# Batch 0 of an attention and snake-MLP kernel: the last pair's V by heads, two first-layer tiles opened early, w_in in five loads

## The chip, the cores and the metric

The kernel runs on one core of one Trainium2 chip. A core has TensorE (PE in the profile; PEld are its weight loads), VectorE (DVE), ScalarE (ACT), GpSimd (POOL) and SyncE (SP), and 16 DMA engines. The metric is device microseconds of one execution. The median of three timed runs of the kernel before is 215.98 us (215.56 to 216.43).

## The reference

An attention over short windows, then a feed-forward layer with the snake function, in float32:

```python
# 4 batches, 8 heads, 768 rows, 64 columns a head; 8 memory rows a head
for c in range(24):                       # chunks of 32 rows
    q_c    = q[:, :, 32*c : 32*c+32]
    k_full = concat(mem_k, k[:, :, max(0, 32*c-16) : min(768, 32*c+40)])
    v_full = concat(mem_v, v[...the same rows...])
    a = softmax(q_c @ k_full.T / 8)
    out[:, :, 32*c : 32*c+32] = a @ v_full
x = out.transpose(0, 2, 1, 3).reshape(3072, 512)
h = x @ w_in                              # 512 -> 2048
g = h + sin(alpha * h)**2 / (alpha + 1e-9)
return g @ w_out                          # 2048 -> 512
```

## The kernel before

Matmuls are in bfloat16. One program works through the four batches, 768 rows each, in five stages. Stage -1 does the attention of batch 0 alone. Stage i (0 to 3) does the feed-forward layer of batch i and beside it the attention of batch i+1. There is no planner at run time: the order of the whole program is written out by hand as strings of short words, and `Stage.run` (L525) calls for each word the method `do_` and its first letter. Each engine gets its instructions in this order and works through them in order; the waits between engines come from the data and the buffers.

The words that matter here, for batch 0 (its attention works by pairs of heads, 0 to 3, and by halves of 384 rows):

- `Vbhk` (L637, `load_v` L160): POOL issues the loads of V of batch b, heads h to k-1, into `vw`: L172 for 64 rows and L179 for 56 rows of each window of 96 queries, with 8 windows ("blocks") a head; for head 0 of batch 0 also L168. `dm` (L665) loads mem_v; `m0` copies it into `vw` (L188).
- `sph` (`u_scores`, L314): scores of pair p, half h: two matmuls for the mask (L317), eight for q·k (L325), then one exp on ACT (L332) into one of eight `pt` buffers.
- `vph` (`u_values`, L339): eight matmuls of the weights with V (L344), for two heads and four windows; then `normed` (L350): a reciprocal (L353) and one multiplication (L354, 96x512) on DVE into a slot `x_blk`.
- `Tph` or `tph` (`turned`, L362): four transposes on TensorE (L366) and a copy into `xT` (L369), on ACT for `T` and on DVE for `t`.
- `Ws` (`warm`, L698): a one-element Sin on ACT (L699), which makes it load the Sin table there.
- `Ixy` (`load_w_in`, L212): POOL issues the load of w_in for the first-layer tiles x to y-1 (digits above 9 as letters, g is 16), 128 columns a tile, 128 KB a tile as stored; the instruction is at L213. `Uxy` does the same for w_out (L219); `dq108`, `dk108` load q and k of batch 1 (L155).
- `bn`, `hn` (L546, L552): the two halves of first-layer tile n, four matmuls each (`half_tile`, L422, the instruction is L424), one for each 128 rows of w_in; the row block kt of w_in goes with pair kt of `xT`. `h` then has ACT take the Sin (L439). `qnE`: the square on ACT (L444), DVE or POOL (L447). `gn`: DVE makes the tile of `gT` (L451), and the tile's two PSUM banks are given back.
- `pn`, `Pn` (L540, L543, `early` L533): open tile n with the matmuls of kt 0 to 2 alone, for the first and the second half; a later `b` and `h` do what is left. The strings of before do not use them.
- `fn`: n matmuls of the second layer (L462) from a feed; `zn`: n matmuls of zeros (L686) that have no use as data.

PSUM has eight banks, handed out by `Banks` (L59): a score tile, a value tile and a first-layer tile take two neighbours, a transposed tile one; the oldest ones given back are taken first. So four first-layer tiles fill it, and the fifth waits for the first `g`.

In stage -1 before, the pairs come in the order 1, 0, 3, 2. V of the last pair (heads 4 and 5) is loaded by `V046`, after `m0`.

Of the kernel before, what the change touches and what calls it, by code (L numbers as in the profile page):

```python
# [9 lines left out]
P = 128  # L10
QW = 96
# [4 lines left out]
F32 = mybir.dt.float32  # L16
ACTF = mybir.ActivationFunctionType
ALU = mybir.AluOpType
# [67 lines left out]
def kernel(  # L86
# [12 lines left out]
    nc = tc.nc  # L99
    B, H, S, D = q.shape  # L100
# [4 lines left out]
    HP = H // 2  # L105
# [3 lines left out]
    HALF = S // 2  # L109
# [6 lines left out]
    blk = ctx.enter_context(tc.tile_pool(name="blk", bufs=3))  # L116
# [4 lines left out]
    banks = Banks(ps)  # L121
# [11 lines left out]
    vws = [consts.tile([P, H, NJ, VP], BF, name=f"vw{i}") for i in range(2)]  # L133
    xslots = Slots([consts.tile([QW, HP, 2, D], BF, name=f"x_blk{i}") for i in range(6)])
# [204 lines left out]
    def u_values(b, hp, half, pt):  # L339
        ot, bs = banks.pair()  # L340
        otv = ot[:, :, 0:4 * (D + 1)].rearrange("p e (g c) -> p e g c", c=D + 1)
        for e in range(2):
            for i in range(4):
                nc.tensor.matmul(  # L344
                    otv[:, e, i, :], pt[:, HALF * e + QW * i:HALF * e + QW * i + P],
                    vws[b % 2][:, 2 * hp + e, 4 * half + i, 0:D + 1],
                )
        return normed(otv, bs)

    def normed(otv, bs):  # L350
        rinv = blk.tile([QW, 2, HP], F32, name="rinv")
        x_blk = xslots.take()
        nc.vector.reciprocal(rinv[:], otv[0:QW, :, :, D])  # L353
        nc.vector.tensor_tensor(  # L354
            out=x_blk[:].rearrange("p g e d -> p e g d"), in0=otv[0:QW, :, :, 0:D],
            in1=rinv[:].unsqueeze(3).to_broadcast([QW, 2, HP, D]),
            op=ALU.mult,
        )
        banks.give(bs)
        return x_blk  # L360

    def turned(x_blk, out, eng):  # L362
        bank, bs = banks.single()
        xtp = bank[:, 0:2 * QW].bitcast(BF).rearrange("p (g c) -> p g c", g=4)
        for g in range(4):
            nc.tensor.transpose(  # L366
                xtp[:, g, :], x_blk[:, g].rearrange("p e d -> p (e d)"), ident[0:QW, 0:QW]
            )
        copier(eng)(out, xtp)  # L369
        banks.give(bs)  # L370

    def u_turn(xT, hp, half, x_blk, eng="V"):
        turned(
            x_blk,
            xT[:, hp, HALF * half:HALF * half + HALF].rearrange("p (g c) -> p g c", g=4), eng)
# [32 lines left out]
    def values(b, j, pt):  # L408
        ot, bs = banks.pair()
        otv = ot[:, :, 0:4 * (D + 1)].rearrange("p e (g c) -> p e g c", c=D + 1)  # L410
        for e in range(2):
            for hp in range(HP):
                i = 4 * e + hp
                nc.tensor.matmul(  # L414
                    otv[:, e, hp, :], pt[:, QW * i:QW * i + P],
                    vws[b % 2][:, 2 * hp + e, j, 0:D + 1],
                )
        return normed(otv, bs)
# [84 lines left out]
    class Stage:  # L503
# [99 lines left out]
        def do_v(self, a):  # L603
            if self.b == 0:
                self.xb[a] = u_values(0, int(a[0]), int(a[1]), self.pt.pop(a))
            else:
                self.xb[a] = values(self.b, int(a), self.pt.pop(int(a)))

        def turn_x(self, a, eng):
            x = self.next_x()  # L610
            x_blk = self.xb.pop(a)
            if self.b == 0:
                u_turn(x, int(a[0]), int(a[1]), x_blk, eng)
            else:
                turned(x_blk, x[:, :, QW * int(a):QW * int(a) + QW], eng)
            xslots.give(x_blk)
# [186 lines left out]
    def const_s():  # L803
# [7 lines left out]
    stage = Stage(-1, None)  # L811
    stage.tile = first
    stage.run((
        'a1A Cb Cp Cz Cv a5A eVA Cm Cl z4 a0V Ci k0 dm a4V l0 k1 K0V Ck l1 L0A V024 We L1V a2A K1A V002 '
        'a6V k2 s00 K2V a3V s11 V068 m0 a7V s01 l2 s10 k3 K3A L2A V046 z4 v10 l3 Cs L3A I02 v11 s20 z1 '
        'v01 s30 z1 v00 s31 z1 v30 s21 v31 T01 T10 v20 T30 T00 v21 T20 T31 I27 t11 t21 eVA Ws '
    ))
    for i, words in enumerate(((
        'o8 b0 h0 I7g q0V U69 U12 b1 h1 dq108 q1A b4 h4 b3 g0 h3 b6 g1 dk108 q4V g4 q3A b2 h2 h6 b5 h5 '
        'Ufg g3 b7 q2V U01 U56 q6P h7 g2 q5A b10 U24 q7P g6 h10 b9 q10A g5 h9 U45 b8 h8 g7 g10 q8A q9V '  # L820
        'V158 b11 h11 g9 b13 g8 h13 l0 l2 l3 L0A L2A q13P k2 q11V Ube b15 U9b g11 Uef g13 K2V h15 b12 '
        'q15V h12 q12A b14 g15 f7 h14 V125 k1 k0 g12 l1 K1V k3 L1V L3A q14V K3A K0A V102 f9 g14 s61 f16 '
        'm1 s70 s3 f13 v0 f3 v6 c6 f6 v3 f5 s542 T3 f10 T0 v4 f6 v2 f2 v1 c4 c2 f7 v7 f1 T1 f3 v5 Ws T7 '
        'f8 t5 '
    ),(
        'b0 o1 h0 b3 R2 q0V h3 b1 Ws q3A g0 g3 h1 q1V b2 R4 h2 q2A b5 h5 b4 h4 Ws g1 g2 q5V g5 b6 q4A h6 '
        'R8 Ws g4 b8 q6A g6 h8 R1 b9 q8V dy h9 b7 q9A g8 Z h7 R3 V378 b11 h11 b10 g9 V226 h10 R4 q7V Ws '
        'q10A f2 X8 q11A g7 f8 b12 h12 g10 g11 b14 h14 q12P g12 b13 h13 V202 q13A g13 q14A f7 X6 b15 g14 '
        'h15 f7 eV We s24 q15V f6 g15 f7 V268 s05 s1 f1 m2 f14 v4 v1 f6 v0 f1 v2 f2 c4 f6 s63 s7 t1 f4 c2 '
        'v6 V357 T0 f4 v3 f4 v7 c7 v5 t3 f17 t5 T6 '  # L830
    ),(
        'b3 Ws R9 b0 h0 R1 h3 b5 h5 Ws R1 b1 q5A q0V g0 R2 q3P g3 h1 Ws q1A b2 h2 g5 R1 g1 b4 h4 R1 b6 '
        'q4A q2V h6 g2 R1 Z b7 h7 b9 h9 R1 g4 R2 q6V b8 g6 R1 eV o1 h8 q7P g7 q8A b11 h11 X1 q11A q9P b10 '
        'g9 g8 h10 b13 g11 h13 q10V g10 b14 h14 b12 q13P X3 V305 h12 g13 q12V q14A R1 f8 eAV b15 g12 '
        'R1 H3 h15 f6 g14 q15V X8 s24 f16 g15 f2 s103 f9 v4 v0 f3 X1 f2 X1 c4 v3 f2 c3 v2 f1 c2 f6 c0 '
        's675 f10 v1 f4 c1 Ws f1 v7 v5 c7 v6 f2 c6 c5 f24 '
    ),(
        'b2 h2 q2V b0 h0 b4 q0A g2 h4 b3 h3 g0 o2 b1 h1 Ws q3P b6 q4V q1A h6 g4 b8 h8 g3 b5 g1 q6A h5 q5A '
        'b7 g6 h7 b11 q8P g8 h11 b10 g5 q7V h10 q10A q11P b9 h9 q9A g7 g11 b12 h12 b15 g10 q12A h15 g9 '
        'g12 b13 h13 b14 q15A h14 g15 q14A q13V g14 g13 '  # L840
    ))):
        stage = Stage(i, stage.nx).run(words)
    feed.take(400)
# [29 lines left out]
```

## Time and profile before

| of the profiled execution | |
|---|---|
| its own time | 214.84 us |
| span of the program in the trace | 213.1 us |
| PE, PEld busy | 201.7 and 113.5 us |
| DVE, ACT, POOL busy | 140.5, 143.5, 99.8 us |
| granted TensorE clock | 1.0 of full speed |
| first of V of the last pair issued (V046, L172) | 14.34 us |
| V of the last pair landed | 22.15 us |
| first first-layer matmul (L424) | 24.81 us |
| Sin table load (ACT, L699) | 25.05 us, 1.28 long |
| first Sin, first gT (L439, L451) | 26.45 and 28.86 us |
| loads of w_in: issue to landing | 256 KB 4.6, 640 KB 7.9, 1152 KB 12.6 us |

Times within the execution are microseconds from the span's start. A line of a timeline has the start, the length, the engine, the line of the kernel, the operation, output and input with their sizes, how many of them follow each other, and in brackets how long the engine stood idle before and what released it. The chain of work that ended last is followed back from the last instruction, at each step to what released it; its lines have start, length, engine and what was made. "issue" in it is time in which the engine waited for nothing that the profile shows. A matmul's length in the trace is from its start until its result stands; the next one can start sooner. KB of a load are those written on the core.

### The profile page before, as it was taken

To read this page: it belongs to the slowest core of one execution; us is meant where nothing else is said; L and a number is where in the kernel's file an instruction comes from. 1 tells how busy PE (TensorE), PEld (TensorE's weight loads), DVE (VectorE), ACT (ScalarE), POOL (GpSimd) and SP (SyncE) were. 2 spreads that over 40 slices of the span, in tenths; PEclk is the share of its full clock that TensorE was granted. 3 is DMA by queue.
4 is the path that set the end of the run, shared out by engine and by line. 5 is a ranking of instruction groups with operands and counts; after the bars stand their busy time and mean duration, and the time that the engine had idled before them with its cause. 6 is when DMAs were issued, how large, how long until landed. Compare 5 with 4: busy or idle time off the path is not lost.

```text
span 213.1 us, 4479 instructions
## 1 busy us (share of the span) xinstructions
PE 201.7 (95%) x1721; PEld 113.5 (53%) x1721; DVE 140.5 (66%) x218; ACT 143.5 (67%) x230; POOL 99.8 (47%) x140
## 2 busy tenths in 40 slices
PE   0799899999999999999999999999999999999994
PEld 0456555565455556555455555554555555554443
DVE  7598678999542749975856649898157197865011
ACT  2597898976857469977846199887846289891110
POOL 8959515688598193009991039659400023200000
PEclk9999999999999999999999999999999999999999
DMA  6999999999999999969999229989945400000312
GB/s 195 337 163 141 193 209 205 204 163 182 131 177 141 137 148 144 180 88 110 126 217 171 72 63 131 156 126 129 175 115 123 124 15 0 2 3 0 148 49 98
DMA packets 95908, 28.19 MB, mean 132 GB/s; under 512 B 84864, under 2 KB 92432, under 8 KB 95888
## 3 DMA queue, kind: packets, MB, share of 16 engines
q0 software_dynamic: 68736, 13.25, 92.3%
q1 hardware_dynamic: 26976, 14.62, 28.2%
q8 instruction: 13, 0.21, 0.4%
q14 instruction: 7, 0.06, 0.1%
q10 hardware_dynamic: 176, 0.04, 0.1%
HBM read 29.66 MB, written 6.29 MB: 169 GB/s over the span
## 4 chain that ended last, share of the span: by engine, by line
PE 71%; DVE 9%; DMA 7%; ACT 4%; issue 4%; POOL 3%; DVEq 0%; POOLq 0%; ACTq 0%
PE ps L462 38%; PE ps L424 27%; DMA memv_st<-in_mem_v_dram 4%; DVE gT L451 4%; DVE s L447 3%; DMA vw<-in_v_dram 3%; PE ps L414 3%; PE ps L385 2%; ACT u L439 2%; PE ps L366 1%; ACT s L444 1%; POOL s L447 1%; POOL vw L172 1%; DVE kT L285 1%; ACT L699 1%
## 5 line engine op out<-in xcount | busy, mean ns | idle before, releaser
L462 PE MATMUL ps<-w_out_sb,gT 128*128 128x512 bf16 (+2 forms) x400 | 89.1, 371 | 0.0
L424 PE MATMUL ps<-xT,w_in_sb 128*128 128x384 bf16 x512 | 86.0, 326 | 0.7 <-DVE gT L451 0.4
L451 DVE SCALAR_TENSOR_TENSOR gT<-s,inv_alpha,ps 128x768 bf16<-128x768 f32 x64 | 63.0, 1011 | 12.5 <-ACT s L444 5.2
L424 PEld LDWEIGHTS <-w_in_sb 128*128 128x128 bf16 x512 | 49.8, 98 | 35.4 <-issue 2.1
L439 ACT ACTIVATE u<-ps,alpha_sb 128x768 f32<-128x768 f32 x64 | 56.6, 895 | 16.8 <-PE ps L424 14.3
L462 PEld LDWEIGHTS <-gT 128*128 128x128 bf16 x400 | 36.6, 98 | 37.9 <-DVE gT L451 0.2
L447 POOL TENSOR_TENSOR s<-u 128x768 f32<-128x768 f32 x11 | 17.4, 1582 | 69.7 <-ACT u L439 69.7
L399 ACT ACTIVATE pt<-ps,biasm 128x256 bf16<-128x256 f32 x72 | 27.2, 489 | 10.5 <-PE ps L385 10.5
L469 DVE COPY o_sb<-ps 128x512 f32<-128x512 f32 (+1 forms) x15 | 10.1, 678 | 28.3 <-PE ps L462 26.4
L447 DVE TENSOR_TENSOR s<-u 128x768 f32<-128x768 f32 x23 | 21.9, 953 | 7.8 <-ACT u L439 7.8
L444 ACT ACTIVATE s<-u 128x768 f32<-128x768 f32 x30 | 25.0, 841 | 0.5
L354 DVE TENSOR_TENSOR x_blk<-ps,rinv 96x512 bf16<-96x512 f32 x32 | 22.0, 687 | 1.1
L469 ACT COPY o_sb<-ps 128x512 f32<-128x512 f32 (+1 forms) x10 | 5.6, 562 | 21.6 <-PE ps L462 21.6
L172 POOL DMA_DIRECT2D vw<-in_v_dram x13 | 12.9, 994 | 7.9 <-PE ps L366 5.4
L353 DVE RECIPROCAL rinv<-ps 96x8 f32<-96x8 f32 x32 | 6.4, 200 | 13.5 <-PE ps L414 12.7
L179 POOL DMA_DIRECT2D vw<-in_v_dram x13 | 12.7, 976 | 0.0
L238 POOL DMA_DIRECT2D kst<-in_k_dram x16 | 12.2, 760 | 1.1 <-DMA vw<-in_v_dram 0.8
L232 POOL DMA_DIRECT2D kst<-in_k_dram x16 | 11.3, 708 | 2.3 <-DMA vw<-in_v_dram 1.6
L369 ACT COPY xT<-ps 128x384 bf16<-128x384 bf16 x12 | 5.6, 496 | 8.2 <-PE ps L366 8.2
L245 POOL DMA_DIRECT2D q_bf<-in_q_dram x12 | 10.7, 912 | 0.0
L414 PEld LDWEIGHTS <-pt 128*128 128x128 bf16 x192 | 8.2, 97 | 4.2 <-ACT pt L399 0.3
L414 PE MATMUL ps<-vw,pt 128*128 128x65 bf16 x192 | 8.9, 193 | 0.0
(81 smaller groups left out, 131.4 us busy)
## 6 DMA issues: line engine op xcount, KB each, us to landing
out_dram<-o_sb SPq DMA_DIRECT2D x23, 256.0 KB, 2.3
kq_f<-in_k_dram SPq DMA_DIRECT2D x4, 384.0 KB, 6.5
kq_f<-in_q_dram SPq DMA_DIRECT2D x4, 384.0 KB, 6.0
q_bf<-in_q_dram POOLq DMA_DIRECT2D x12, 128.0 KB, 6.7
w_in_sb<-in_moe_w_in_dram POOLq DMA_DIRECT2D x1, 1152.0 KB, 12.6
vw<-in_v_dram POOLq DMA_DIRECT2D x7, 128.0 KB, 6.7
vw<-in_v_dram POOLq DMA_DIRECT2D x8, 112.0 KB, 7.4
kst<-in_k_dram POOLq DMA_DIRECT2D x14, 64.0 KB, 5.1
```

The lines of the kernel that those rows point to most:

```text
L172: nc.gpsimd.dma_start(vw[0:64, lo:c1, 0:D], win(vflat, a, n, 64))
L179: nc.gpsimd.dma_start(vw[72:128, c0:hi, 0:D], win(vflat, base + QW * c0 + 48, hi - c0, 56))
L354: nc.vector.tensor_tensor(out=x_blk[:].rearrange("p g e d -> p e g d"), in0=otv[0:QW, :, :, 0:D], in1=rinv[:].unsqueeze(3).to_broadcast([Q ...
L399: nc.scalar.activation(pt[:, 0:H * QW].rearrange("p (g e c) -> p g e c", g=2, e=4)[:, :, :, 32 * m:32 * m + 32], sc[:, :, 0:4 * QW].rearra ...
L414: nc.tensor.matmul(otv[:, e, hp, :], pt[:, QW * i:QW * i + P], vws[b % 2][:, 2 * hp + e, j, 0:D + 1],)
L424: nc.tensor.matmul(t["hT"][:, hf, 0:HALF], w_in_sb[:, kt, P * t["ft"]:P * t["ft"] + P], t["xT"][:, kt, HALF * hf:HALF * hf + HALF], start= ...
L439: nc.scalar.activation(t["u"][:], t["hT"][:, :, 0:HALF], ACTF.Sin, scale=alpha_sb[:, ft:ft + 1])
L444: nc.scalar.activation(s2[:], u[:], ACTF.Square)
L447: e.tensor_tensor(out=s2[:], in0=u[:], in1=u[:], op=ALU.mult)
L451: nc.vector.scalar_tensor_tensor(out=gT[:, ft, :].rearrange("p (e c) -> p e c", e=2), in0=t["s2"][:], scalar=inv_alpha[:, ft:ft + 1], in1= ...
L462: nc.tensor.matmul(o[:, c0:c1], gT[:, ft, P * s:P * s + P], w_out_sb[:, ft, c0:c1], start=(ft == 0), stop=(ft == FT - 1),)
L469: copier(state["engines"][state["o"] % len(state["engines"])])(o_sb[:, c0:c1], o[:, c0:c1])
```

## The change

Stage -1 and the loads of w_in are ordered anew; stages 1 to 3 are the same words, broken into lines in another way.

- The last two pairs are exchanged: V of heads 4 and 5 is loaded where heads 6 and 7 were (`V046` ahead of `m0`), and pair 3 is now the last.
- V of pair 3 is loaded head by head, `V067` and `V078`: four loads of 8 blocks in place of two of 16.
- Its values are made head by head by a new word `w` (`head_values`): eight matmuls for one head and both halves, one reciprocal, and two multiplications of 96x256, one into the slot of each half.
- First-layer tiles 0 and 1 are opened with the row blocks of pairs 0 to 2 (`p0 P0`, `p1 P1`), ahead of and behind the transposes of pair 3.
- Pair 3's two transposes come last, `T30` on ACT after the table load `Ws`, and `t31` on DVE; `T11` and `T21` are on ACT now.
- w_in comes in five loads, `I02 I24 I47 I7b Ibg` (256, 256, 384, 512 and 640 columns), in place of `I02 I27 I7g` (256, 640 and 1152).

```diff
+    def head_values(b, hp, e, pt_of, x_of):
+        ot, bs = banks.pair()
+        otv = ot[:, :, 0:4 * (D + 1)].rearrange("p m (g c) -> p m g c", c=D + 1)
+        for half in range(2):
+            for i in range(4):
+                nc.tensor.matmul(
+                    otv[:, half, i, :], pt_of[half][:, HALF * e + QW * i:HALF * e + QW * i + P],
+                    vws[b % 2][:, 2 * hp + e, 4 * half + i, 0:D + 1],
+                )
+        rinv = blk.tile([QW, 2, HP], F32, name="rinv")
+        nc.vector.reciprocal(rinv[:], otv[0:QW, :, :, D])
+        for half in range(2):
+            nc.vector.tensor_tensor(
+                out=x_of[half][:, :, e, :], in0=otv[0:QW, half, :, 0:D],
+                in1=rinv[:, half, :].unsqueeze(2).to_broadcast([QW, HP, D]),
+                op=ALU.mult,
+            )
+        banks.give(bs)
...
+        def do_w(self, a):
+            hp, e = int(a[0]), int(a[1])
+            names = [a[0] + str(half) for half in range(2)]
+            if e == 0:
+                for n in names:
+                    self.xb[n] = xslots.take()
+            head_values(0, hp, e, [self.pt[n] for n in names], [self.xb[n] for n in names])
...
-        'a6V k2 s00 K2V a3V s11 V068 m0 a7V s01 l2 s10 k3 K3A L2A V046 z4 v10 l3 Cs L3A I02 v11 s20 z1 '
-        'v01 s30 z1 v00 s31 z1 v30 s21 v31 T01 T10 v20 T30 T00 v21 T20 T31 I27 t11 t21 eVA Ws '
+        'k2 s00 K2V a3V s11 V046 m0 a7V s01 l2 s10 k3 K3A L2A V067 z4 v10 V078 l3 Cs L3A I02 v11 s20 z1 v01 '
+        's21 z1 v00 s30 z1 T01 T10 v20 s31 T00 v21 T11 T20 w30 T21 w31 Ws I24 I47 p0 P0 T30 t31 p1 P1 eVA '
...
-        'o8 b0 h0 I7g q0V U69 U12 b1 h1 dq108 q1A b4 h4 b3 g0 h3 b6 g1 dk108 q4V g4 q3A b2 h2 h6 b5 h5 '
+        'o8 b0 h0 I7b q0V Ibg U69 U12 b1 h1 dq108 q1A b4 h4 b3 g0 h3 b6 g1 dk108 q4V g4 q3A b2 h2 h6 b5 h5 '
```

## What was predicted

> **What bounds the kernel now.** I read the page's busy times and 40 slices first, then the chain of work that ended last in order of time, then the timeline of each engine from 14 to 36 us, the landings of the single loads, and the waits. Durations below come from the profiled execution: span 213.1 us, 214.84 us in all, so 1.7 us lie around the span. The median of the three timed runs is 215.98 us, 1.14 us more; I work out a difference and add it to that median.
>
> ```profile
> PE 201.7 (95%) x1721; PEld 113.5 (53%) x1721; DVE 140.5 (66%) x218; ACT 143.5 (67%) x230; POOL 99.8 (47%) x140
> PE   0799899999999999999999999999999999999994
> ```
>
> TensorE is busy 95% of the span, and from the sixth slice on without a gap that one can see. Time can be won or lost only ahead of that, or where TensorE is held up. The chain shows what sets its start:
>
> ```profile
> 16.09 6.06 DMA vw<-in_v_dram
> 22.15 0.14 issue
> 22.29 0.43 PE ps L344 x8
> ...
> 24.55 0.48 ACT xT L369
> 25.03 0.02 issue
> 25.05 1.28 ACT L699
> ...
> 26.35 0.20 ACT tiny L699
> 26.55 0.79 ACT u L439
> 27.34 0.02 issue
> 27.36 0.97 DVE s L447
> ...
> 28.38 0.48 issue
> 28.86 0.07 DVE gT L451
> ...
> 29.79 1.01 DVE gT L451
> ...
> 35.74 1.30 PE ps L424 x7
> ```
>
> Here V of heads 4 and 5 lands at 22.15; its products, the last xT copies, the load of the Sin table and the first Sin (26.45 in the timeline) follow. From then to 35.7 VectorE holds the chain: a product tile's PSUM banks come free only with its gT (L451), so the fifth and sixth tile wait for the first and second gT. TensorE is not the limit there. A change of the start therefore counts by what it does to **the first two gT, at 28.86 and 29.79**, not by the matmuls that it moves.
>
> **Part 1, V by heads, pairs 3 and 2 exchanged.** The built program gives POOL's loads eight semaphores in turn; a load waits for the one eight places before it. Before, the ninth load (V of the last pair) waited for mem_v (landed 14.06) and started at 14.34; the waits view has it as "POOL vw L172 <- DMA memv_st", 2.5 us. After, the same wait stands in front of head 6's load. Four half loads replace two: a V load of 16 blocks takes 0.90 us to issue and one of one block 0.56 (L168, 7.68), so 8 blocks take some 0.72, and the four end near 18.05 where the two ended at 16.97. The rows are the same, and the loads landed 0.9 to 1.1 us apart (20.14, 21.05, 22.15 for the last three), so head 6 should have landed by 21.1 and head 7 by 22.2. Pair 2's V now lands at 20.14. The landing wait of 22.15 goes. What is late next is **ScalarE**, whose order is now: exp of pair 3 half 0, copies T01 and T10, exp of half 1, copies T00, T11, T20, T21, table load, T30.
>
> ```profile
> 19.99 0.81 ACT L332 ACTIVATE pt<-ps 128x768 bf16<-128x768 f32 x1 [0.20 <-PE ps L325]
> 21.18 0.81 ACT L332 ACTIVATE pt<-ps 128x768 bf16<-128x768 f32 x1 [0.38 <-PE ps L325]
> 21.89 0.86 ACT L369 COPY xT<-ps 128x384 bf16<-128x384 bf16 x2
> ```
>
> An exp lets the next instruction start after 0.71 us (21.18 to 21.89), a copy after 0.38 (two take 0.86, one 0.48). From 19.99 on: T01 at 20.70, T10 at 21.08, the second exp at 21.46 (its scores need the banks of the first exp, free at 20.80, plus 0.55 as from 20.63 to 21.18, so 21.38: no wait), T00 from 22.17 to 22.65. The second half of head 6's products is written where T00's bank was: 22.68 to 23.02. So head 6 is *not* earlier than the pair was (22.29).
>
> VectorE then has two reciprocals (0.20) and four multiplications of 96x256 instead of two and two of 96x512 (0.69). No row shows 96x256. Bounds: 0.20 (96x8, L353) and 0.69; I take 0.44, halfway, since the size is halfway. One head: 0.24 + 0.40 + 0.44 = 1.08. Two from 23.05: **25.2**, against 24.58 before. That is +0.6 us on the last pair.
>
> **Part 2, two tiles opened on three pairs.** Twelve of the 128x384 matmuls move ahead, at 0.163 us from start to start (eight in 1.47 from 24.81, the last 0.33 long). Tile 0's six wait for the copy of T20 (its banks; 22.93 to 23.41) and run from 23.42 to 24.4, beside VectorE's work: free, if the first w_in load has landed. Tile 1's six stand behind the transposes of t31, which wait for 25.2: four transposes 0.17, then 25.40 to 26.38. Then tile 0's last two, ending at 26.38 + 0.16 + 0.33 = 26.87: **first Sin at 26.9, not 26.45: +0.45**. The table load is hidden now (23.84 to 25.14, T30's copy to 25.74), but it was only 0.1 us later than tile 0 before (25.95 + 0.33 = 26.28). Tile 1 is whole at 27.2, before 27.57, so the second Sin goes at 26.9 + 0.85 = 27.75 (+0.1) and its square at 28.7 (+0.1). TensorE can start its third tile at 26.87 and not 27.41; this lead of 0.54 ends in a wait for the banks of the first gT.
>
> First gT: square of tile 0 from 27.8 to 28.77, then 28.85. Before it stand 0.48 us of "issue" for which no view gives a cause (the next gT after a square on VectorE follows within 0.1: 31.67 to 31.77). It is the first instruction of its kind in the program, and POOL is idle, so I leave it in place: 29.33 against 28.86, **+0.45**, the second at 30.25 (+0.45). From there VectorE, then TensorE, carry it to the end; no view shows slack that would take it back.
>
> **Part 3, w_in in five loads.** Each is 0.76 us of POOL (18.03, 18.81, 19.54); the first starts some 1.07 later (19.1). V keeps the queues full until its last landing, so the first lands at 22.7 to 23.4 (4.6 from issue before, 22.66), hidden until 23.42, and behind that until tile 0's six no longer fit ahead of 24.8. The third tile needs the third load, up to the same column block range as the second before (26.72): 896 KB in both. It is wanted at 26.87 and costs nothing until 28.0, since the tile must end only for the Sin slot near 29.4. The two memsets of kst (L804, L805) move 1.07 later on POOL too; their tile is first read from 50 us on. Two w_out loads (U01, U56) now wait for the third and fourth w_in load, to some 26.8 and 29.5 instead of 23.9 and 27.0; they land behind K and Q at 43 to 44 either way, and POOL's next square is at 34.18: free. K and Q of batch 1 and w_out stand two loads later in the queue; k_bf landed at 42.46 and is used at 43.4, now 43.9.
>
> What does a load cost beyond its bytes? Nothing by seven that were queued behind each other: w_out 384 KB 1.91 us, 128 KB 0.65, Q and K 768 KB 3.87 and 3.86, w_out 0.64, 0.64, 0.67, all 197 to 205 KB/us. Between w_in's second and third (median engine: 640 KB 3.58, 1152 KB 5.55) a line gives 1.1 us a load. I take 0 to 0.2, by the seven; the other end is a rival. By the Trainium skill (DMA: Bandwidth & Descriptors, Anatomy of one DMA) each such load has a fixed 2.0 us; paid in series for two more loads k_bf would be at 46.5, 2.6 us behind its use, and the sum 219.0. The seven landings above, 0.65 us apart for 128 KB, speak against paying it in series.
>
> **Sum.** +0.45 from the start, nothing from the loads: 214.84 + 0.45 = 215.3 for a profiled execution, 215.98 + 0.45 = **216.4** as a median. A run tells about 0.5% (1.1 us) from no change.
>
> **Rivals.**
> - *The start comes out even.* The 0.48 us of issue are gone, or the 96x256 multiplications are shorter (0.33 each would give 0.4 back). The first gT is then at 28.86 as before: **216.0**. For it: nothing ties that gap to the instruction. Against: nothing else is busy there.
> - *The last V landing was worse in the timed runs.* They are 1.14 us above the profiled one, and V's landing is the one load on the chain behind 14 us. The changed kernel takes a head 7 that is 1.0 us late (wanted at 23.2) without loss. If all 1.14 are V's, the change wins 1.0 and loses 0.45; with short multiplications as well it passes -1.1: **215.0** (-1.0). Against: the three runs spread by only 0.87.
> - *The load queue becomes the bound (the other side).* At 1.1 us a load, k_bf lands at 42.46 + 2.2 = 44.7 against 43.9: 0.8 more, **217.2**. It decides when k_bf lands after 43.9, or the third w_in load after 28.0; then the transposes of batch 1's K (L274) stop TensorE.
> - *It does not do what it says:* the opened tiles start no earlier. In the built program tile 0's stand ahead of the last transposes and tile 1's right behind, and neither reads pair 3; only their use is lost, which is my forecast.
>
> **Chances.** Forecast 0.44, even 0.22, V's landing 0.16, queue 0.18. Faster by over 0.5%: half of V's case and a little of the even one, 0.10. Slower: two thirds of the queue's case and a tail of the forecast (multiplications at 0.55 or more), 0.18. Within: 0.72. The range takes the even case, the larger part of V's case and the queue's price: 215.2 to 217.4. With the multiplication at its ends (0.20, 0.69) the first Sin would move by -0.9 and +1.0; nearer to the middle row the range has it.
>
> **What would show it.** Right: no TensorE wait for vw in front of the last products; first Sin at 26.7 to 27.1; second head's multiplications ending near 25.2; first gT near 29.3; TensorE idle 0.3 to 0.6 ahead of the fifth or sixth tile. Wrong: last xT done before 25.3 and a Sin before 26.4 (then it is faster); TensorE waiting for w_in_sb or k_bf (queue); the first gT at 28.9 or before (even); a 96x256 multiplication outside 0.36 to 0.50.

## The result, and the profile after

The kernel after takes 218.87 us (median of 217.45, 217.68, 220.06 and 221.21), the kernel before 216.09 beside it (215.56 to 216.43): ratio 1.0122, 95% interval 1.0078 to 1.0166, so some 2.6 us slower. The ratios here and below leave out runs more than 1.5% above the fastest of their kernel, here the one of 221.21. I had said 216.4 (215.2 to 217.4). The profiled execution is the one of 221.21 us, with a span of 219.1; it is 6.0 us longer than that of before, and not all of this is in every run. From the page, the lines that answer to those of before, with the granted clock:

```profile
PE 203.0 (93%) x1702; PEld 114.6 (52%) x1721; DVE 140.6 (64%) x219; ACT 143.7 (66%) x231; POOL 101.6 (46%) x144
PE   0899889999999999999999999995999999999993
PEclk9999999999999999999999999998899999999999
```

TensorE has as much to do, and two holes: a small one in the sixth slice (27 to 33 us) and a large one in the 28th (148 to 153 us), which before did not have, with a lower clock just behind it. To see where time goes I took the ends of the 64 gT instructions (their order is the same in both) and subtracted those of before:

| | us against before |
|---|---|
| 1st gT of batch 0 | -0.14 |
| 7th to 16th gT of batch 0, and all of batches 1 and 2 | +0.85 |
| all of batch 3 | +5.09 |
| end of the span | +6.00 |

So there are three places: between the first and the seventh gT, near 150 us, and behind the last gT. The rest of the program has the same pace to 0.01 us.

**The start.** Lines of ScalarE's timeline, then of VectorE's:

```profile
23.99 1.28 ACT L726 ACT_TABLE_LOAD   x1
...
26.72 1.69 ACT L458 ACTIVATE u<-ps,alpha_sb 128x768 f32<-128x768 f32 x2 [0.87 <-PE ps L443]
29.98 0.90 ACT L458 ACTIVATE u<-ps,alpha_sb 128x768 f32<-128x768 f32 x1 [0.69 <-PE ps L443]
```

```profile
23.33 0.75 DVE L362 TENSOR_TENSOR x_blk<-ps,rinv 96x256 bf16<-96x256 f32 x2
24.23 0.75 DVE L362 TENSOR_TENSOR x_blk<-ps,rinv 96x256 bf16<-96x256 f32 x2
27.65 0.96 DVE L466 TENSOR_TENSOR s<-u 128x768 f32<-128x768 f32 x1 [1.88 <-ACT u L458]
28.72 1.94 DVE L470 SCALAR_TENSOR_TENSOR gT<-s,inv_alpha,ps 128x768 bf16<-128x768 f32 x2
```

The first Sin is 0.27 later than before (26.72 against 26.45), yet the first gT is 0.14 earlier: the square ends at 28.61, gT starts at 28.72, and the 0.48 us of "issue" is not there (e9 and e10 below show what it hangs on). But the third Sin, at 29.98, waits for TensorE, which waits for a load. TensorE's timeline and the chain of work that ended last:

```profile
23.55 1.14 PE L443 MATMUL ps<-xT,w_in_sb 128*128 128x384 bf16 x6
25.22 1.79 PE L443 MATMUL ps<-xT,w_in_sb 128*128 128x384 bf16 x10
28.47 3.75 PE L443 MATMUL ps<-xT,w_in_sb 128*128 128x384 bf16 x22 [1.46 <-DMA w_in_sb<-in_moe_w_in_dram]
```

```profile
18.21 0.55 POOL kst L831
...
18.80 0.52 POOL kst L832
19.32 1.46 POOL w_in_sb L213 x2
20.77 7.65 DMA w_in_sb<-in_moe_w_in_dram
...
28.47 2.61 PE ps L443 x15
```

The load in the chain is the third of w_in (I47). It lands at 28.42, where before had as many bytes of w_in by 26.72, and k_bf lands at 44.34 instead of 42.46. In the trace each load adds 16 increments to a semaphore, and a wait ends with the last of them: here half of them had come by 27.23, before by 25.34, and the last 1.2 and 1.4 us behind that. The DMA lines of two stretches, 19 to 21 us and 23 to 27 us, first before, then after:

```profile
DMA packets 1292, 0.28 MB, mean 141 GB/s; under 512 B 948, under 2 KB 1292, under 8 KB 1292
DMA packets 511, 0.83 MB, mean 207 GB/s; under 512 B 16, under 2 KB 335, under 8 KB 510
```

```profile
DMA packets 1013, 0.13 MB, mean 66 GB/s; under 512 B 961, under 2 KB 1013, under 8 KB 1013
DMA packets 916, 0.60 MB, mean 150 GB/s; under 512 B 27, under 2 KB 916, under 8 KB 916
```

Two losses. At 19 to 21 us V had all but landed (its last at 21.51, before 22.15), and the first w_in load, issued 1.24 later, was not there yet: 0.15 MB not moved. At 23 to 27 us the same engines moved 916 packets of 0.66 KB where before moved 511 of 1.6 KB: 0.23 MB less. Between the two, at 21 to 23 us, both moved alike (0.33 and 0.32 MB). Together 0.38 MB, at 0.205 MB a us 1.9 us, which is what k_bf is late. In this profile only the first of the two late loads costs time: all of the +0.85 stands by the seventh gT, and K's transposes, which read k_bf, start at 44.38 and add nothing to it. By the Trainium skill (DMA: Bandwidth & Descriptors, Why small descriptors are slow) every descriptor carries a fixed overhead; the 150 against 207 GB/s agree in direction.

**Near 150 us.** Windows and chain of the kernel after:

```profile
145.00:150.00 5.00, 2.80 (x22) 1.31 (x20) 4.04 (x5) 3.39 (x5) 4.96 (x7) 1.00 3.02 130
150.00:155.00 5.00, 4.84 (x21) 2.01 (x23) 0.00 (x0) 1.21 (x3) 2.52 (x5) 0.66 2.19 67
```

```profile
143.48 6.54 DMA qT<-q_bf
...
150.16 0.35 PE ps L404 x8
```

The first number behind the stretch's length is PE's busy time, the 0.66 the granted clock. The last transpose of q for batch 3 is in flight for 6.54 us (before 3.9: 142.38 to 146.29), TensorE stands 2.35 us for it, and then works at half its clock from 151.5 to 154.9: 4.24 us in all. The Trainium skill (TensorE: Matmul & The Clock Gate, Part 1) gives windows of 3413 ns at half or full rate; the trace has one of 3.41 us.

**The end.** The span goes on 3.44 us behind the last output copy (before 2.53). The DMA issue line of the last output load, before and then after; its last number is the median time to landing:

```profile
out_dram<-o_sb SPq DMA_DIRECT2D x1, 64.0 KB, 1.6
```

```profile
out_dram<-o_sb SPq DMA_DIRECT2D x1, 64.0 KB, 2.5
```

Of the 16 increments of the last load 15 come at their usual time and one 0.9 us later. In the trace an 8 KB transfer of an instruction queue starts 2.27 us ahead of the span's end; before, such a transfer starts 0.64 behind it.

### The profile page after: what moved, and what is told of

It reads as the page before. It is cut to its first block, busy times and chain, and to the rows that moved or that the text cites. A ratio compares the mean times of both kernels' runs of the same rounds, so it can differ in the third digit from the quotient of the medians.

```text
span 219.1 us, 4467 instructions
## 1 busy us (share of the span) xinstructions
PE 203.0 (93%) x1702; PEld 114.6 (52%) x1721; DVE 140.6 (64%) x219; ACT 143.7 (66%) x231; POOL 101.6 (46%) x144
## 4 chain that ended last, share of the span: by engine, by line
PE 66%; DMA 12%; POOL 6%; SPq 5%; DVE 4%; issue 3%; ACT 2%; POOLq 0%; DVEq 0%; ACTq 0%
PE ps L481 36%; PE ps L443 24%; DMA memv_st<-in_mem_v_dram 4%; DMA w_in_sb<-in_moe_w_in_dram 3%; DMA qT<-q_bf 3%; PE ps L433 3%; SPq L260 2%; PE ps L404 2%; SPq L263 2%; DVE gT L470 2%; DMA kst<-in_k_dram 2%; ACT u L458 1%; POOL s L466 1%; POOL vw L172 1%; PE ps L385 1%
## 5 line engine op out<-in xcount | busy, mean ns | idle before, releaser
L458 ACT ACTIVATE u<-ps,alpha_sb 128x768 f32<-128x768 f32 x64 | 56.5, 895 | 18.3 <-PE ps L443 15.8
L418 ACT ACTIVATE pt<-ps,biasm 128x256 bf16<-128x256 f32 x72 | 27.3, 488 | 11.4 <-PE ps L404 11.3
L373 DVE TENSOR_TENSOR x_blk<-ps,rinv 96x512 bf16<-96x512 f32 x30 | 20.6, 686 | 1.0
L172 POOL DMA_DIRECT2D vw<-in_v_dram x14 | 13.4, 956 | 7.9 <-PE ps L385 5.0
L179 POOL DMA_DIRECT2D vw<-in_v_dram x14 | 13.2, 940 | 0.3 <-DMA q_bf<-in_q_dram 0.3
L388 ACT COPY xT<-ps 128x384 bf16<-128x384 bf16 x13 | 6.1, 504 | 7.7 <-PE ps L385 7.7
```

Source lines behind the costliest of these rows:

```text
L172: nc.gpsimd.dma_start(vw[0:64, lo:c1, 0:D], win(vflat, a, n, 64))
L179: nc.gpsimd.dma_start(vw[72:128, c0:hi, 0:D], win(vflat, base + QW * c0 + 48, hi - c0, 56))
L373: nc.vector.tensor_tensor(out=x_blk[:].rearrange("p g e d -> p e g d"), in0=otv[0:QW, :, :, 0:D], in1=rinv[:].unsqueeze(3).to_broadcast([Q ...
L418: nc.scalar.activation(pt[:, 0:H * QW].rearrange("p (g e c) -> p g e c", g=2, e=4)[:, :, :, 32 * m:32 * m + 32], sc[:, :, 0:4 * QW].rearra ...
L458: nc.scalar.activation(t["u"][:], t["hT"][:, :, 0:HALF], ACTF.Sin, scale=alpha_sb[:, ft:ft + 1])
```

## The experiments

Theory Q: the load queue is late for the two reasons above, and holds TensorE at two gates, the third w_in load and k_bf. Rivals: the new start loses by itself; or only the third load counts. Theory R: the wait for qT is a race of the transposes with batch 3's last V loads. Theories I and D: the end is set by the length of an engine's instruction stream. Each table gives the median and the ratio to the kernel before beside it, with its 95% interval.

### The queue

e1, the kernel after with three loads:
```diff
-w31 Ws I24 I47 p0 P0
+w31 Ws I27 p0 P0
...
-h0 I7b q0V Ibg U69
+h0 I7g q0V U69
```


> The kernel after, with w_in in three loads again (256, 640 and 1152 columns). Theory Q (the queue of POOL's loads is the loss: it runs 1.9 us late, 1.1 of it because the two loads of 256 columns move 125 to 168 GB/s between 23 and 27 us where before moved 193 to 220, 0.75 because the first is issued 1.24 later and leaves the DMA engines idle at 20 to 21 us): the load for the third tile lands near 27.3 instead of 28.42, TensorE's wait for it falls from 1.46 to 0.2 to 0.5 us, k_bf lands at 43.1 to 43.5 instead of 44.34, and the time is 216.0 to 216.7. Rival S (the new start itself loses, by values head by head and tiles opened early; what TensorE waits for w_in it would else wait for PSUM banks): 217.2 to 217.8, as the kernel after.

e2, the kernel before with five loads:
```diff
-T20 T31 I27 t11
+T20 T31 I24 I47 t11
...
-h0 I7g q0V U69
+h0 I7b q0V Ibg U69
```


> The kernel before, with w_in in five loads in the places that the kernel after gives them, and nothing else. Theory Q: the queue ends 1.1 us later than before, so the third load lands near 27.8 and TensorE waits 0.2 to 0.5 us for it ahead of the third tile; k_bf lands near 43.5 where it was used at 43.46. 216.3 to 217.0. Rival S: the split costs nothing by itself, 215.8 to 216.2, and no wait for w_in_sb.

e3, the kernel after with tiles 2 and 4 exchanged:
```diff
-b4 h4 b3 g0 h3 b6 g1 dk108 q4V g4 q3A b2 h2
+b2 h2 b3 g0 h3 b6 g1 dk108 q2V g2 q3A b4 h4
...
-g3 b7 q2V U01 U56 q6P h7 g2
+g3 b7 q4V U01 U56 q6P h7 g4
```


> The kernel after, with first-layer tiles 2 and 4 exchanged in the order of batch 0, so that the third tile reads the second load of w_in (landed at 26.48) and not the third (28.42). Theory Q says that the whole queue is late, not one load: the wait of 1.46 us goes and the third Sin is at 29.2 to 29.5 instead of 29.98, but k_bf still lands near 44.3 and would now be wanted at 43.5, so TensorE waits some 0.8 us ahead of K's transposes of batch 1 and the time stays at 217.0 to 217.6. Rival T (only the third tile's load matters): no wait for k_bf, 216.2 to 216.7.

e4, the kernel after with the memsets of kst later:
```diff
-l3 Cs L3A I02 v11
+l3 L3A I02 v11
...
-Ibg U69 U12
+Ibg Cs U69 U12
```


> The kernel after, with the two memsets of kst moved on POOL from ahead of the first load of w_in to behind the fifth, so that the loads are issued 1.07 us earlier. Theory Q: all five land 0.7 to 1.1 us earlier (third near 27.5), TensorE's wait is 0.4 to 0.8, k_bf near 43.5, 216.4 to 216.9. Rival: the loads are bound by V's packets ahead of them and not by their issue: third load at 28.2 or later, 217.2 to 217.8.

| | median us | runs | ratio |
|---|---|---|---|
| e1_three_loads | 216.82 | 12 | 1.0057 (1.0024 to 1.0090) |
| e2_split_only | 215.79 | 12 | 1.0011 (0.9979 to 1.0043) |
| e3_tile_order | 219.64 | 6 | 1.0147 (1.0088 to 1.0207) |
| e4_memsets_later | 220.49 | 6 | 1.0160 (1.0087 to 1.0232) |

None of the four medians lies where theory Q had put it: e1 is 0.1 us above its range, e2 at the rival's 215.8, and e3 and e4 are 2.0 and 3.6 us above theirs. Four runs of six of e3, and four of e4, are at 219.6 and more. The profiled one of e4 (220.09) has a stall of 2.60 us near 150 us; that of e3 was a run of 217.15, so what its high runs have is not on record. The profiles tell more than the medians.

e3 is the clearest. The wait for w_in is gone, the gT of batch 0 are 0.26 ahead of before, and then the second gate takes it all; its 16th gT is at +0.63, batch 1 at +0.91. Its chain:

```profile
24.98 19.32 DMA k_bf<-in_k_dram
...
44.34 0.53 PE ps L274 x12
```

In e1 the load for the third tile landed at 28.37 and not near 27.3, and TensorE waited for it as long as in the kernel after:

```profile
28.42 1.80 PE L443 MATMUL ps<-xT,w_in_sb 128*128 128x384 bf16 x10 [1.56 <-DMA w_in_sb<-in_moe_w_in_dram]
```

k_bf landed at 44.20, hardly sooner. The medians of the 16 increments did come sooner, at 26.67 against 27.23 and at 42.68 against 43.35 after, and at 23 to 27 us 0.73 MB were moved where after moved 0.60; but the last increments lagged 1.7 and 1.5 us behind the median ones. So in the profile the larger loads alone are worth 0.6 to 0.7 us at the median increment, and the lag of the last hides all of it. e1's time is below that of the kernel after, but the intervals of the two ratios overlap: that the small packets are a part of the loss is made likely by e1 and not shown. e2 says that five loads cost the old start little, 0.2 us with an interval that holds zero, as the rival had it; in its profile V was late, the first gT at +1.59, and a late start hides late loads. e4's third load landed at 27.60, near the 27.5 of theory Q and not at the rival's 28.2 or later, and TensorE did not wait for it; but k_bf landed at 44.11 and not near 43.5, and what the loads were worth in time can't be read, since TensorE ran at half rate from 12.4 to 15.8 us and the first gT came at +1.06. That is a further scatter. e7 below has it too (first gT at +2.57); its window of 12 to 16 us, where before has a clock of 1.00:

```profile
12.00:16.00 4.00, 3.74 (x59) 2.77 (x61) 3.35 (x7) 2.91 (x5) 1.07 (x1) 0.57 2.92 152
```

Nor is the old start free of the two gates. e5 below has the start of before, word for word; in its profile the second w_in load landed at 28.12 and k_bf at 44.75, their last increments 2.4 and 2.75 us behind the median ones, TensorE waited 0.50 and 0.60 us for them, and batch 1 is at +1.77. And in the five profiles with the loads and the tile order of the kernel after (after, e6, e7, e10, e13) the stretch from the first gT to batch 1 cost 0.99, 0.30, 0.53, 0.04 and 0.82 us. What the queue costs thus differs from run to run; 0.85 is the figure of one profile.

### The end and the race

e5, the kernel before with one more instruction on ScalarE, and e6, the kernel after with one less:
```diff
-b0 o1 h0 b3 R2             # e5
+b0 o1 h0 Ws b3 R2
-b1 Ws q3A g0               # e6
+b1 q3A g0
```


> The kernel before, with one more one-element Sin (L699) on ScalarE in stage 1, behind the first Sin there, where ScalarE is idle 0.40 us. In all four kernels that have the new start the span goes on 3.44 us behind the end of the last copy, where it was 2.52 in the two that have the old one: one of the 16 increments of the last output load comes 0.9 us after the others, and an 8 KB transfer of the instruction queue starts 2.28 us ahead of the span's end, where it started 0.64 behind it. Theory I: this is ScalarE's instruction stream, one instruction longer in the new start (seven copies of xT in place of six), which crosses a fetch boundary sooner. Then this kernel, with nothing else changed, has 3.4 us behind the last copy and is 0.9 us slower than before: 216.0 to 216.5 against 215.3. Rival: it is VectorE's stream (two instructions longer) or the start itself: 2.52 us, and no change.

> The kernel after, with one of the one-element Sins taken out (L726, in stage 1, where the Sin table is in place already), so that ScalarE has as many instructions as in the kernel before. Theory I (ScalarE's instruction fetch at the end): 2.5 us behind the last copy instead of 3.44, and 0.9 us faster than the kernel after: its undisturbed runs at 216.5 instead of 217.5, 1.2 above the kernel before. Rival (VectorE's stream or the start): 3.44 us, 217.5.

e7, the kernel after with the last V later, and e8, the kernel before with it earlier:
```diff
-q13P X3 V305 h12 g13 q12V q14A R1 f8 eAV b15 g12 R1 H3 h15     # e7
+q13P X3 h12 g13 q12V q14A R1 f8 eAV b15 g12 R1 V305 H3 h15
-b12 q13P X3 V305 h12                                           # e8
+b12 V305 q13P X3 h12
```


> The kernel after, with the loads of batch 3's last V (heads 0 to 4, V305) moved on POOL from ahead of two q loads to behind them, some 1.8 us later (issued at 144.9 instead of 143.1). Theory R (a race): the runs at 219.6 to 222 are those in which the fourth transpose of q is issued a few tenths later (142.38 in before and in e3_tile_order, no wait; 142.57 to 142.94 in the others, shifts taken out, waits of 1.2 to 2.7) and its packets fall behind this V's on the DMA engines; TensorE then stands 1.2 to 2.7 us and its granted clock falls to 0.66 for a while. With V later there is no wait for qT<-q_bf, last gT at +0.9 and not at +5, and all runs lie at 217.0 to 218.0. Rival (the transposes are late by themselves, or by the q loads): runs above 219 as in the kernel after.

> The kernel before, with the same V loads moved one POOL square ahead (issued near 137.3 instead of 142.23), so that they lie in front of more of the transposes of k and q of batch 3. Theory R: the transposes land later, TensorE waits for qT or kT by 1 us or more near 147 in nearly every run, and most runs are at 217 to 221, as only 3 of 23 of the kernel before were. Rival (V's packets have nothing to do with it): as before, most runs at 214.5 to 216.5, or faster since the loads are out of the way by 142.

e9, the kernel before with two more instructions on VectorE, and e10, the kernel after with two less:
```diff
+    nc.vector.memset(spare[:], 0.0)     # e9, twice, behind h0 of stage 1
-    nc.vector.memset(tiny[:], 0.0)      # e10
-    nc.vector.memset(mcol[:], 0.0)
+    nc.gpsimd.memset(mcol[:], 0.0)
```


> The kernel before, with two one-element memsets on VectorE in stage 1, where it is idle. With ScalarE's instruction count set to that of the other kernel in both directions, the 3.44 and 2.53 us behind the last copy stayed where they were, so theory I in its first form has fallen. Theory D: it is VectorE's instruction stream, 324 instructions with the new start and 322 with the old. Then this kernel has 3.4 us behind its last copy, and is 0.9 us slower than before. Rival (the end depends on the start in another way): 2.53 us, no change.

> The kernel after with 322 instructions on VectorE: the memset of a tile that nothing reads is left out, and the memset of mcol is on GpSimd. Theory D: 2.53 us behind the last copy instead of 3.44, and all runs 0.9 us faster than those of the kernel after: the best ones at 216.0 to 216.6. Rival: 3.44 us, 217 and more.

| | median us | runs | ratio | behind the last copy |
|---|---|---|---|---|
| e5_before_one_more_act | 216.07 | 11 | 0.9997 (0.9962 to 1.0032) | 2.54 us |
| e6_after_one_act_less | 218.16 | 11 | 1.0093 (1.0053 to 1.0134) | 3.45 |
| e7_last_v_later | 218.08 | 5 | 1.0106 (1.0032 to 1.0180) | 3.46 |
| e8_last_v_earlier | 221.15 | 5 | 1.0239 (1.0179 to 1.0299) | 2.53 |
| e9_before_two_dve_more | 216.20 | 11 | 1.0025 (1.0000 to 1.0049) | 3.45 |
| e10_two_dve_less | 216.33 | 11 | 1.0032 (1.0002 to 1.0063) | 2.52 |

Theory I fell in both directions, theory D held in both: with 324 instructions on VectorE the end is 0.92 us longer, with 322 it is not, whatever the start. (These are the counts that the expectations use; the traces have rows for 322 and 320 of them, the same two apart.) The last output load of e9, then of e10:

```profile
out_dram<-o_sb SPq DMA_DIRECT2D x1, 64.0 KB, 2.5
```

```profile
out_dram<-o_sb SPq DMA_DIRECT2D x1, 64.0 KB, 1.6
```

A kernel of the one start has the end of the other. In all 18 profiles of this study it is 3.44 to 3.47 us with 324 (seven of them) and 2.52 to 2.54 with 322. That the 8 KB transfer delays the one increment is argued from their times; that the count sets the end is shown, for these two counts. The Trainium skill (Runtime: NRT & Kernel Launch, Instruction fetch mechanics) has the refill of an engine's instructions "mostly hidden"; if that transfer is such a refill, it is not hidden here, beside the last output load. In time e9 is 0 to 1.1 us slower than the kernel before, which holds 0.92 and does not show it by itself.

The count has a second effect, which I had overlooked: it moves the gap of 0.48 us ahead of the first gT. From the end of the square to the first gT there are 0.52 to 0.54 us in 12 of the 18 profiles, and in each of these the first gT is VectorE's 64th row in the trace, its semaphore instructions counted. In the other six (after, e1, e3, e4, e6, e7) it is the 66th, and there are 0.11 us. e9, whose two memsets stand behind the first gT, has the gap as before; e10, with two instructions less ahead of it, has it back in the new start. VectorE's timeline of e9, then of e10:

```profile
29.56 1.94 DVE L452 SCALAR_TENSOR_TENSOR gT<-s,inv_alpha,ps 128x768 bf16<-128x768 f32 x2 [0.53 <-DVE s L448]
```

```profile
30.00 1.94 DVE L470 SCALAR_TENSOR_TENSOR gT<-s,inv_alpha,ps 128x768 bf16<-128x768 f32 x2 [0.53 <-PE ps L443]
```

So the gap hangs on the instruction's place in VectorE's stream, not on its kind and not on the start; why that place is late, no view tells. The two instructions more win 0.42 us at the first gT and cost 0.92 at the end, and the six kernels with the new start that take two out again (e10, e11, e13 to e16) have the gap again and the shorter end.

e8 supports theory R: V's loads five us earlier (137.19; the two q loads behind them 2.5 earlier) bring the stall into the profile, and all five runs are as long (220.86 to 221.9). From its waits view (us in total, times, longest):

```profile
PE ps L385 <- DMA qT<-q_bf: 4.8, 2, 3.3
```

In e7's profile, with V later and the same q loads earlier, there is no wait for qT, as expected, but two of its five runs are above 219, the profiled one through the late start told above, so not all lie at 217.0 to 218.0, as theory R had it. So the runs above 219 have at least two causes. Nor is V's place the whole of it: e6 and e10, with V where it was, had one such run in 22.

### What is left, and the repairs

e11 has the edits of e3, e7 and e10, e12 that of e7, and both load q and k of batch 1 ahead of w_out (the lines of e11):
```diff
-U69 U12 b1 h1 dq108 q1A b2 h2 b3 g0 h3 b6 g1 dk108 q2V
+b1 h1 dq108 q1A b2 h2 b3 g0 h3 b6 g1 dk108 U69 U12 q2V
```


> The kernel after with a repair for each of the three losses: VectorE at 322 instructions (theory D: 2.53 us at the end), batch 3's last V behind the two q loads (theory R: no wait for qT), and for the load queue (theory Q) the third tile reads the second load of w_in (tiles 2 and 4 exchanged) and q and k of batch 1 are loaded ahead of two loads of w_out (512 KB, 2.55 us), so that k_bf lands near 41.8 against 43.4 where it is used. If these three are all, what is left is the new start, first gT 0.1 to 0.3 ahead of before: 214.9 to 215.6, 0 to 0.5 us faster than the kernel before. If the start has a loss of its own: 216 or more.

> The kernel before, with the repairs of the last V and of the load queue (q and k of batch 1 ahead of two loads of w_out) alone. Theories R and Q: nothing binds in its undisturbed runs, 214.8 to 215.4, but the runs above 217 get fewer. Against e11 it tells what the new start is worth by itself: by the first gT 0.1 to 0.3 us for it, by the rival that the new start has a loss of its own this kernel is 0.5 us or more ahead.

e13 is the kernel after with the edits of e7 and e10; e14 is e13 with that of e3; e16 is e13 with `I27` for `I24 I47`, `I7g Cs` for `I7b Ibg`, and `Cs` taken out ahead of `I02`. e15 is e11 with
```diff
-q8A q9V V158 b11 h11 g9
+q8A q9V b11 h11 g9
...
-L0A L2A q13P k2
+L0A L2A q13P V158 k2
```


> The kernel after with VectorE at 322 instructions and batch 3's last V behind the two q loads. Theory: 2.5 us at the end and no wait for qT in the profile; what is left against before is the load queue, 0.3 to 0.9: 215.8 to 216.8, and no run above 218 save for a late V in the start. Rival: runs at 219 and more stay, as many as in the kernel after.

> As e13, and tiles 2 and 4 of batch 0 exchanged, so that the third tile does not read the third load of w_in. Theory Q (two gates of the same late queue): the wait for w_in_sb goes, but the one for k_bf (lands near 44.3 against 43.5 wanted) takes its place: within 0.2 us of e13. If the third load were all of it: 0.5 to 0.8 us faster than e13.

> The kernel e11_after_repaired lost 0.9 us at 43 to 46 us, since a load of V (V158) on GpSimd, now in front of a later place in the queue, waited for the load of w_out eight places before it (landed 43.72), and GpSimd's square and its gT stood behind it. Here V158 is moved behind that square. Theory: neither w_in nor k_bf nor this gates TensorE, scores of batch 1 at 53.4 to 53.8 instead of 54.76; 215.0 to 215.9. If the new start has a loss of its own: 216.3 or more, as e11.

> As e13, but w_in in three loads (256, 640, 1152 columns) that are issued ahead of the two memsets of kst, some 1.1 us earlier. Theory Q: the load of the third tile lands near 27.0 and k_bf near 43.0 to 43.3, so that neither costs more than 0.2 us; 215.2 to 216.0, 0.4 to 0.8 faster than e13. Rival (the new start): as e13.

| | median us | runs | ratio |
|---|---|---|---|
| e11_after_repaired | 216.84 | 12 | 1.0054 (1.0034 to 1.0074) |
| e12_before_two_repairs | 216.29 | 12 | 1.0001 (0.9967 to 1.0035) |
| e13_v_later_dve | 216.86 | 12 | 1.0056 (1.0031 to 1.0081) |
| e14_tile_order_v_dve | 217.14 | 9 | 1.0075 (1.0050 to 1.0100) |
| e15_repaired_v158 | 219.35 | 6 | 1.0169 (1.0121 to 1.0218) |
| e16_three_memsets | 216.08 | 12 | 1.0029 (0.9997 to 1.0062) |

e13 and e14 against each other are theory Q's two gates: e13 waits 1.2 us for w_in, e14 not at all, but 1.04 for k_bf (its timeline), and it is no faster.

```profile
45.38 0.53 PE L274 MATMUL ps<-ident,k_bf 128*64 128x128 bf16 x12 [1.04 <-DMA k_bf<-in_k_dram]
```

No run of e13 is above 218, as expected; its median is 0.1 us above its range, and e14's is 0.28 above that, where 0.2 at most was expected. e16, which relieves the whole queue, is 0.78 us below e13 in the median, the size that theory Q had; its interval holds the kernel before, but the two kernels' runs spread over 2.1 and 3.7 us and their intervals overlap, so this difference is not clear of noise. In its own profile V was late and the first gT at +1.81; the third tile's load landed at 29.01, which cost a wait of 0.52, and k_bf at 44.92, so the landings I had named can't be judged there.

e11 missed its 214.9 to 215.6 by over 1 us. k_bf landed at 41.83, as worked out, and TensorE waits for neither load, but the gap ahead of the first gT is back (its first gT is at +0.30), and the gate moved a third time. GpSimd's timeline:

```profile
42.68 0.98 POOL L172 DMA_DIRECT2D vw<-in_v_dram  x1 [3.63 <-DMA k_bf<-in_k_dram]
44.01 1.01 POOL L179 DMA_DIRECT2D vw<-in_v_dram  x1 [0.35 <-DMA w_out_sb<-in_moe_w_out_dram]
45.03 1.48 POOL L466 TENSOR_TENSOR s<-u 128x768 f32<-128x768 f32 x1
```

A V load waits for the load eight places ahead, the square behind it is late, and its gT 0.92. e15 moved V, and the next load in the queue became the gate, w_out in 49.25 to 56.85 ("DMA w_out_sb", 7.59 us in its chain): a miss, and the worst of the repairs. e12 says that the repairs bring the old start nothing (216.29, where 214.8 to 215.4 was expected); its runs above 217 are fewer (1 of 12, against 9 of 35 of the kernel before), which can be chance. It is 0.55 us ahead of e11, the mark that I had set for a loss of the new start by itself; since e11 has 0.92 at its V load, that loss is neither shown nor ruled out. No version beat the kernel before.

## Why the prediction was wrong, step by step

- **The bound** (the first two gT) was read rightly for the start, and it is no longer the bound after: the loads are.
- **Part 1.** Right: head 6 no earlier (products 22.49 to 22.98 against 22.29). The 96x256 multiplication takes 0.41 to 0.42, near the 0.44 assumed, but the next instruction starts after 0.34, not 0.40; VectorE was done at 24.98, not 25.2.
- **Part 2.** The order came as worked out: tile 0's six at 23.55 (23.42), table load 23.99 to 25.27 (23.84 to 25.14), first Sin 26.72 (26.9). The 0.48 us of issue that I left in place, as those of the first instruction of its kind, were absent: they hang on the place in VectorE's stream, and the new start puts two more instructions ahead. So the first gT was at 28.72 and not 29.33 (0.42 of it by the gap, 0.18 by the Sin): the forecast's +0.45 became -0.14, the even rival's condition. For that rival I had written that nothing ties the gap to the instruction, which was right; that the change itself would remove it I did not see. Against the profile of before, the first gT is at +0.05 to +1.59 in five more profiles of the old start and at -0.29 to +2.57 in twelve of the new, by V's landing, the clock at 12 us and the gap; so what the new start is worth by itself is not settled; it is no large gain.
- **Part 3 is the step that failed.** "V keeps the queues full until its last landing" was wrong: they ran nearly dry at 20 to 21 us (44 GB/s). And "what does a load cost beyond its bytes ... I take 0 to 0.2, by the seven": those seven were of long rows; the loads of 256 columns move 0.66 KB packets, and my line between two w_in loads (1.1 a load) was the better row. The third load landed at 28.42 and not at 26.7. The threshold (nothing until 28.0) was about right: 0.42 behind it, the third Sin was 0.68 late (29.98 against 29.30). With k_bf at 44.34 instead of 43.9 this is the queue rival, with its mechanism and the two loads that it names; I gave it 0.18. That its price agrees (0.8 said, 0.85 measured) is luck in part: it was priced at k_bf, on top of +0.45, while here the third load cost all of it, behind a first gT at -0.14, and k_bf nothing. In e3 and e14, where the third load does not bind, k_bf does (waits of 0.95 and 1.04).
- **The sum lacked a term.** 0.92 us at the end, by two instructions more on VectorE (324 against 322). I had counted the instructions and given their number no price. Nothing in the profile before points to the end; the gap ahead of the first gT was its other sign, and I took it for that instruction's own.
- **The rest.** 0.85 and 0.92 make 1.8 us, 217.9 on the median of before, and the two lower runs are at 217.45 and 217.68. The two higher ones are 2.4 and 3.5 above these; in the profiled one it is the stall near 150 us (4.24). I called TensorE's later stages free of slack, but did not look at what slack the loads there have: the last transpose landed 146.29, for scores at 146.61. Whether the change makes this stall more frequent stays open: the kernel before shows runs above 217.3 as well, 22 of its 105 runs beside the experiments, 13 of them above 219.

## What to carry to other kernels

A load is late by more than its bytes: look for microseconds in which the queue moves little between the issue and the first packet, and compare the size of the packets, not of the loads. When a queue is late, taking away the wait at one load moves it to the next one (w_in, then k_bf, then V and w_out here); price the whole queue against every use. And after a change, compare the time behind the last copy and the gaps that no view explains: an engine's instruction count can move both.

## What I had not expected of the hardware

Two instructions more on VectorE cost 0.92 us at the end of the program, in every profile, and where they stand ahead of the first gT a gap of 0.42 us there is gone. A wait of 2.35 us on TensorE cost 4.24, since a window of 3.41 us at half the clock followed; waits of 2.34 in e2 and 2.60 in e4 cost 2.9 and 2.8 and had no such window, so the length of the wait alone does not bring it. And the last of a load's 16 increments came 0.5 to 3.3 us behind their median through the second to the last load of w_in, in the profiles of both starts; a wait ends with the last.
